# Last parts of experts in quarters of a block, three shared blocks in place of four, in a fused attention and mixture-of-experts kernel

## The chip, the cores and the metric

One core of a Trainium2 chip runs the whole program. The metric is the device time of one execution in microseconds; a profiled execution gives the span from the first to the last instruction and the time of each instruction. Engines are called TensorE (PE; its weight loads are the row PEld), VectorE (DVE), ScalarE (ACT), GpSimd (POOL) and the queue of SyncE (SP).

## What is computed

Two steps are joined. The first is a linear attention with a sketched polynomial kernel, for 4 batches, 4 heads, 1088 positions and a head size of 32: with `phi(x)` the 64 products of two 8-number sketches of `x`, each position gets `phi(q) (sum phi(k) v) / (phi(q) sum phi(k) + 1e-6)`. The heads of a position side by side are a row of 128 numbers, and there are 4352 rows.

The second step sends each row to one of 8 experts:

```python
logits = xn @ en.T / tau                     # xn, en: rows and expert embeddings of length 1
expert_idx = np.argmax(logits, axis=1)
gate_w = probs[np.arange(N), expert_idx]     # probs: softmax of the logits
for e in range(E):
    mask = expert_idx == e
    h = np.maximum(x[mask] @ w1[e], 0.0)     # 128 -> 1024
    out[mask] = gate_w[mask, None] * (h @ w2[e])   # 1024 -> 128
```

So which rows go to which expert is known only while the program runs.

## The kernel before, in words

**Attention.** Batches are handled in two pairs (`m` = 0, 1). Their rows and logits (136 numbers a row) are written to a scratch area in device memory. The steps of the second pair are laid between the first blocks of the experts.

**Blocks.** The rows of an expert are gathered into blocks of 128 (`fetch`, L927: an indirect DMA that GpSimd issues, with row numbers `dst_i` worked out on the chip) and scattered into the output after the two layers (L1032). A block has one expert, whose first-layer weights (512 KB) SP's queue loads with the expert's number read from memory (`weights`, L949); the second layers of all experts lie in `w2_sb`. Ten blocks (`EARLY`) are planned from the first half of the rows, the rest (`LATE`) when all rows are known.

**Shared blocks.** An expert's rows are rarely a multiple of 128. An expert whose last part has at most 64 rows takes only half a block; blocks with the numbers 30 to 33 (`FULL` = 30, `SHARED` = 4) can hold the halves of two experts. They are computed with both experts' weights: `two(i)` (L956) says which they are, `first_b` and `second_b` are the second expert's weights (the second layer is copied by ScalarE, L971).

- `up(i)` (L976) multiplies the turned block (features x rows) by the first layer. A full block takes 8 matmuls of 128 x 128 x 128, a shared one four per `f`: for each of the two experts (`b`) and each half `c` of the 128 hidden numbers, 64 array columns, moving the 64 rows of that expert (L989).
- `turn(i)` (L934) turns a gathered block on TensorE.
- `down(i)` (L1014) adds up 8 matmuls with 128 hidden numbers each. The block's rows are the array columns here. A shared block takes two per `f`, 64 array columns each, one for each expert (L1023).

Float32 matmuls stand in the profile as two instructions each.

**The plan.** `plan_late` (L848) finds for each expert how many whole blocks it has (`full`, a rounded sum from TensorE) and whether a half is left (`odd`), counts the blocks, gives each block a key, and `table` (L775) turns keys into row numbers: TensorE adds up marks, VectorE reduces them (L817). The rows of second halves are moved down 64 partitions by a small matmul (`halves`, L809).

**Order.** The order is written out by hand. `put_at(tick)(after, rank, f)` puts a step `f` at a tick and a rank in it; `emit` (L1125) issues them so on TensorE, VectorE, ScalarE, GpSimd and SP alike. A tick `i` has `up(i)`, `turn(i + 1)` and `down(i - 1)`, in this order on TensorE (`in_ticks`, L1099). 36 blocks (`USUAL`) are always computed. A conditional part at the end (L1141) computes more, up to `NBLK` = 38, if the count read from memory says so. The profile has 36 gathers (L930), so it was not run.

The lines that the change touches lie in the constants at the top, `more_constants`, `iotas`, the handling of the sketch words (L198 to L216), `plan_late`, `table`, `up` and `down`:

Of the kernel before, what the change touches and what calls it, by code (L numbers as in the profile page):

```python
# [33 lines left out]
NBLK = ((N + E * (HALF - 1)) // HALF + 1) // 2  # L34
# [17 lines left out]
LATE = NBLK - EARLY  # L52
SHARED = E // 2
PAIRS = FULL - EARLY
AHEAD = 4
USUAL = N // P + 2
# [9 lines left out]
def kernel(  # L66
# [131 lines left out]
    def word(name):  # L198
        return consts.tile([2 * R, D], U32, name=name)
    top, rem, w, fits = word("s_top"), word("s_rem"), word("s_w"), word("s_fits")  # L200
# [10 lines left out]
    srow = consts.tile([2 * R, D], F32, name="srow")  # L211
# [3 lines left out]
    srows = consts.tile([2 * R, H, D], F32, name="srows")  # L215
# [30 lines left out]
    before, ones = consts.tile([P, P], BF16, name="before"), consts.tile([P, P], BF16, name="ones")  # L246
    less, more = consts.tile([P, E], BF16, name="less"), consts.tile([P, E], BF16, name="more")
    near = consts.tile([P, E], BF16, name="near")
    down_half = consts.tile([HALF, P], BF16, name="down_half")
    base = consts.tile([P, E], BF16, name="base")  # L250
# [10 lines left out]
    nowhere = [consts.tile([P, 2, n], BF16, name=f"nowhere{n}") for n in (EARLY, LATE + SHARED)]  # L261

    def more_constants():
        nc.vector.memset(ones, 1.0 / P)
        nc.vector.memset(ones_e, 1.0)

        nc.vector.memset(less, -(P - 1) / (2.0 * P))
        nc.vector.memset(more, (P - 1) / (2.0 * P))

        nc.vector.memset(near, -1.0 / (2.0 * P))  # L270
        nc.vector.memset(c_early, 0.0)
        nc.vector.memset(w_late, float(KEYS * E))
        for t in (place_k, place_r):
            nc.vector.memset(t, -1.0)
        for t, n in zip(nowhere, (EARLY, LATE)):
            nc.vector.memset(t, 0.0)
            nc.vector.memset(t[:, 0, :n], float(NOWHERE))

    def iotas():
        li = work.tile([P, P], I32, tag="iota", bufs=2, name="lane_i")  # L280
        nc.gpsimd.iota(li[:], pattern=[[1, P]], base=0, channel_multiplier=0)
        nc.vector.tensor_copy(lane, li)
        part = iota([P, 1], [[1, 1]], 0, 1, "part")
        nc.vector.tensor_scalar(before, lane, part[:, 0:1], 1.0 / P, op0=ALU.is_gt, op1=ALU.mult)
        nc.vector.tensor_scalar(down_half, lane[:HALF], part[:HALF, 0:1], float(HALF), op0=ALU.subtract, op1=ALU.is_equal)
        nc.vector.tensor_scalar_mul(lanes, bview(lane, [[1, P], [0, WIDE]]), 1.0 / P)

        nc.vector.tensor_scalar_mul(prefer, lane[:, :E], -1.0 / (2 * E))  # L290
        nc.vector.tensor_scalar_mul(base, lane[:, :E], float(KEYS))
        tok_i = work.tile([P, 3, NM * NCP], I32, tag="iota", bufs=2, name="tok_i")
        toks = tok_i[:, 0].rearrange("p (m c) -> p m c", m=NM)
        for i in range(2):
            nc.gpsimd.iota(toks[:, :, i * NK:(i + 1) * NK], pattern=[[-2 * S, NM], [-1, NK]], base=NOWHERE - S * i,
                           channel_multiplier=-NK)
        nc.gpsimd.iota(toks[:, :, 2 * NK:], pattern=[[-2 * S, NM], [0, 2]], base=NOWHERE - SK, channel_multiplier=-1)

        nc.vector.tensor_scalar(toks[HALF:, :, 2 * NK:], toks[HALF:, :, 2 * NK:], S - HALF, None, op0=ALU.subtract)
        nc.vector.tensor_scalar(tok_i[:, 1], tok_i[:, 0], ~(P - 1) & 0x7FFFFFFF, None, op0=ALU.bitwise_and)  # L300
        nc.vector.tensor_scalar(tok_i[:, 2], tok_i[:, 0], P - 1, None, op0=ALU.bitwise_and)
        nc.vector.tensor_scalar_mul(digits, tok_i[:, 1:], -1.0)
# [439 lines left out]
    SIZES = (EARLY, LATE)  # L742
# [3 lines left out]
    exp_i = [consts.tile([1, n], I32, name=f"exp_i{i}") for i, n in enumerate((EARLY, LATE + SHARED))]  # L746

    def blocks(which, upto, weight, place):

        n = SIZES[which]  # L750
        le = work.tile([P, n, E], F32, tag="le", bufs=2, name=f"le{which}")
        at = consts.tile([P, n + which * SHARED], F32, name=f"at{which}")[:, :n]
# [22 lines left out]
    def table(which, m1, key):  # L775
# [3 lines left out]
        n, w = SIZES[which] + which * SHARED, m1 * NCP  # L779
# [5 lines left out]
        def find():  # L785
            shape = [P, 3 * w * n]
            both = consts.tile(shape, BF16, name="hits0") if which == 0 else work.tile(
                [P, NC * ROW * 2], BF16, tag="xg0", bufs=1, name="hits1")[:, :3 * w * n]
            s["hit"] = both[:, :w * n].rearrange("p (w n) -> p n w", n=n)
            s["col"] = both[:, w * n:].rearrange("p (w d n) -> p d n w", d=2, n=n)  # L790
            nc.vector.tensor_tensor(out=lie(s["hit"]), in0=lie(key().unsqueeze(2).broadcast_to([P, n, w])),
                                    in1=lie(bview(place_k, [[0, n], [1, w]])), op=ALU.is_equal)
# [12 lines left out]
        def first_rows():  # L805
            s["b"] = consts.tile([HALF, 2, SHARED], BF16, name="halves")
            nc.vector.tensor_copy(s["b"], s["ps"].rearrange("p (d n) -> p d n", d=2)[:HALF, :, LATE:])

        def halves():  # L809

            ps = s["ps"].rearrange("p (d n) -> p d n", d=2)
            nc.tensor.matmul(ps[:, :, PAIRS:PAIRS + SHARED], down_half, s["b"], start=False, stop=True, skip_group_check=True)
# [7 lines left out]
    def tokens_by_expert(rounded, out, ps):  # L820

        for j, r in enumerate(rounded):
            for i, t in enumerate([r] + counts):
                nc.tensor.matmul(ps[:, j * E:(j + 1) * E], ones, t, start=i == 0, stop=i == len(counts))
        nc.vector.tensor_scalar(out, ps, WHOLE, -WHOLE, op0=ALU.add, op1=ALU.add)

    def plan_early():
# [3 lines left out]
        def count():  # L831
            tokens_by_expert((less,), full, spare[0][:, NC * E:(NC + 1) * E])
# [15 lines left out]
    def plan_late():  # L848
# [4 lines left out]
        full, all_ = both[:, :E], both[:, E:]  # L853
        odd, odds, rank, key = column("odd"), column("odds"), column("odd_rank"), column("odd_key")
# [3 lines left out]
        def count():  # L858
            tokens_by_expert((near, more), both, table_bank[0][:, 1, :2 * E])
# [15 lines left out]
        def shared():  # L875

            s["high"] = column("high", w=SHARED)
            nc.vector.tensor_sub(odd, all_, full)
            nc.vector.tensor_tensor_scan(out=odds[:], data0=ones_e[:], data1=odd[:], initial=0.0, op0=ALU.mult, op1=ALU.add)
            nc.vector.tensor_scalar(rank, odd, -(NO_KEY + 1), NO_KEY, op0=ALU.mult, op1=ALU.add)  # L880
            nc.vector.tensor_add(rank, rank, odds)

            nc.vector.tensor_scalar(pairs, odds[:, E - 1:], 0.5, 0.25, op0=ALU.mult, op1=ALU.add)
            nc.vector.tensor_scalar(pairs, pairs, WHOLE, -WHOLE, op0=ALU.add, op1=ALU.add)
            nc.vector.scalar_tensor_tensor(out=key, in0=full, scalar=-NO_KEY, in1=base, op0=ALU.add, op1=ALU.add)
            n = 2 * SHARED
            is_it = work.tile([P, n, E], F32, tag="emb", bufs=2, name="is_it")
            it = work.tile([P, n, E], F32, tag="emb", bufs=2, name="it")
            s["keys"] = column("odd_keys", w=n)
            nc.vector.tensor_tensor(out=is_it, in0=bview(rank, [[0, n], [1, E]]),  # L890
                                    in1=bview(lane, [[1, n], [0, E]]), op=ALU.is_equal)
            nc.vector.tensor_mul(it, is_it, bview(key, [[0, n], [1, E]]))
            nc.vector.reduce_sum(out=s["keys"][:], in_=it, axis=AX.X)

        def others():
# [5 lines left out]
            halves = s["keys"][:].rearrange("p (n u) -> p n u", u=2)  # L901
            late["second"] = column("second_keys", w=SHARED)[0:1]
            late["keys"] = whole
            nc.vector.tensor_scalar_add(whole[:, LATE:], halves[:, :, 1], NO_KEY)

            nc.vector.tensor_tensor(out=late["second"], in0=whole[0:1, LATE:], in1=last[0:1], op=ALU.min)
            nc.vector.scalar_tensor_tensor(out=last, in0=halves[:, :, 0], scalar=NO_KEY, in1=last, op0=ALU.add, op1=ALU.min)
            late["key"] = whole

        def experts():  # L910
# [5 lines left out]
            nc.vector.tensor_scalar_min(exp_i[1], f, float(E - 1))  # L916
            late["n"] = consts.tile([1, 1], I32, name="n_late")
            nc.vector.tensor_add(late["n"], pairs[0:1], upto[0:1, E - 1:])
        return count, rest, shared, others, experts
# [4 lines left out]
    def of(i):  # L924
        return (0, i) if i < EARLY else (1, i - EARLY)
# [32 lines left out]


# [16 lines left out]
    def up(i):  # L976
# [3 lines left out]
        for u in range(2):  # L980
            for j in range(4):
# [4 lines left out]
                for b, wh in enumerate((w, first_b(i))):  # L986
                    for c in range(2):
                        r = slice(c * HALF, (c + 1) * HALF)
                        nc.tensor.matmul(ps[r, u, j * P + b * HALF:j * P + (b + 1) * HALF],  # L989
                                         wh[:, f * P + c * HALF:f * P + (c + 1) * HALF], x[:, b * HALF:(b + 1) * HALF],  # L990
                                         start=True, stop=True)
# [22 lines left out]
    def down(i):  # L1014
# [3 lines left out]
        for f in range(NF):  # L1018
# [3 lines left out]
            for b, w in enumerate(ws):  # L1022
                nc.tensor.matmul(ps[b * HALF:(b + 1) * HALF], h[:, f * P + b * HALF:f * P + (b + 1) * HALF], w[:, f],  # L1023
                                 start=f == 0, stop=f == NF - 1, skip_group_check=True)
# [54 lines left out]
    count, rest, shared, others, experts = plan_late()  # L1079
# [7 lines left out]
    put(2, 75.5, experts)  # L1087
    put(3, 73.5, find)
# [50 lines left out]
    n_late = nc.values_load(late["n"][:, :], min_val=0, max_val=LATE,  # L1139
                            skip_runtime_bounds_check_because="a count of blocks, of which there are no more")  # L1140
    with tc.If(n_late > USUAL - EARLY):  # L1141
        put = put_at(-1)
        for i in range(USUAL, NBLK):
            put(0, 0, lambda i=i: fetch(i))
            if i < USUAL + 2:
                put(0, 1, lambda i=i: weights(i))
        put(0, 2, lambda: turn(USUAL))
        in_ticks(USUAL, NBLK, 0)
# [31 lines left out]
```

## Time and profile before

| | |
|---|---|
| median of 3 runs | 202.54 us (202.13 to 202.78) |
| the profiled execution's own time | 204.43 us |
| its span, first to last instruction | 202.6 us |
| TensorE busy | 192.7 us, 95% of the span |
| VectorE, ScalarE, GpSimd busy | 87.6, 102.4 and 107.0 us |
| share of TensorE in the chain that ended last | 90% |
| granted TensorE clock | 1.0 |
| moved by DMA | 39.42 MB, 195 GB/s on average |

The page gives for each engine the time in which it was busy. The chain of work that ended last is followed back from the last instruction, at each step to what released it or to the instruction before it on its engine; its shares tell which engine set the end. Group lines have the line of the source, the engine, the operation, what it writes and reads, the count, and the mean time of one. A matmul's mean is its latency: matmuls overlap, so that the step from one start to the next, which the timeline shows, is the price of one more.

The blocks of the experts run from 55 us to 198 us of the span, a little under 3.7 us each where they are full. The shared ones run from 171.5 us to 193 us.

### The profile page before, as it was taken

Reading aid. Unit: us, or ns where it says so; the run is one execution under the profiler, and the core shown is the slowest. Engines: PE = TensorE matmul, PEld = TensorE weight load, DVE = VectorE, ACT = ScalarE, POOL = GpSimd, SP = SyncE. Lnnn points to the kernel's source line nnn. Section 1 sums busy time; section 2 is a strip of 40 time slices with the busy share of each in tenths; the row PEclk is TensorE's granted clock in tenths of the full one; section 3 lists DMA queues with packets and bytes.
Section 4 is the critical chain, followed back from the end, with each engine's and each line's share of the span. In section 5 each row is a group of like instructions: output and inputs, shape, how many; then the busy total and the mean of one; then the engine's idle time right before and its main releaser. Section 6 shows DMA issues by size and latency. Waiting matters only on the chain.

```text
span 202.6 us, 6949 instructions
## 1 busy us (share of the span) xinstructions
PE 192.7 (95%) x2586; PEld 182.7 (90%) x2586; DVE 87.6 (43%) x378; ACT 102.4 (51%) x293; POOL 107.0 (53%) x137
## 2 busy tenths in 40 slices
PE   7889999999799999999999999999999999999991
PEld 7667888889689999999999999999999999988991
DVE  6677848888658488912222212222122122112200
ACT  2657451436464456434655546545555465766540
POOL 4000335303813767755878777677676776664043
PEclk9999999999999999999999999999999999999999
DMA  4998799987284886544466665657646784485000
GB/s 132 323 217 287 179 320 293 280 282 208 54 321 139 278 310 211 165 132 145 148 205 189 170 205 155 209 166 163 222 147 184 223 306 169 136 263 190 3 26 25
DMA packets 28162, 39.42 MB, mean 195 GB/s; under 512 B 5738, under 2 KB 21366, under 8 KB 28130
## 3 DMA queue, kind: packets, MB, share of 16 engines
q1 hardware_dynamic: 25776, 34.23, 55.9%
q0 software_dynamic: 2304, 4.74, 7.5%
q8 instruction: 22, 0.36, 0.7%
q14 instruction: 10, 0.08, 0.1%
q10 hardware_dynamic: 50, 0.01, 0.0%
HBM read 34.37 MB, written 4.73 MB: 193 GB/s over the span
## 4 chain that ended last, share of the span: by engine, by line
PE 90%; DVE 4%; ACT 2%; issue 1%; DMA 1%; POOL 0%; POOLq 0%; DVEq 0%
PE ps_big L984 28%; PE ps_ab L1020 14%; PE ps_acc L1020 13%; PE ps_big L613 5%; PE ps_acc L479 4%; PE ps_big L989 4%; PE ps_t L382 3%; PE ps_t L936 2%; PE ps_ab L401 2%; PE ps_big L561 2%; PE ps_acc L1023 2%; PE ps_ab L1023 2%; PE ps_t L802 2%; ACT qpT L570 1%; PE ps_ab L591 1%
## 5 line engine op out<-in xcount | busy, mean ns | idle before, releaser
L984 PE MATMUL ps_big<-xTb,wb 128*128 128x128 f32 x512 | 63.0, 276 | 1.6 <-ACT xTb L938 1.4
L984 PEld LDWEIGHTS ps_big<-xTb,wb 128*128 128x128 f32 x512 | 59.7, 192 | 2.4 <-ACT xTb L938 1.6
L1032 POOL DMA_INDIRECT out_dram<-y,dst_i x36 | 37.7, 1048 | 42.9 <-ACT y L1029 24.4
L992 ACT ACTIVATE hT<-ps_big 128x1024 f32<-128x1024 f32 x36 | 36.9, 1024 | 41.3 <-issue 22.7
L930 POOL DMA_INDIRECT xs<-rows,dst_i x36 | 37.3, 1035 | 18.8 <-DVE dst_i L817 11.3
L938 DVE COPY xTb<-ps_t 128x128 f32<-128x128 f32 x29 | 8.4, 290 | 59.4 <-issue 38.2
L1020 PE MATMUL ps_ab<-w_sb,hT 128*128 x256 | 31.3, 275 | 0.0
L1020 PE MATMUL ps_acc<-w_sb,hT 128*128 x256 | 31.2, 275 | 0.0
L1020 PEld LDWEIGHTS ps_ab<-w_sb,hT 128*128 128x128 f32 x256 | 29.9, 192 | 0.0
L1020 PEld LDWEIGHTS ps_acc<-w_sb,hT 128*128 128x128 f32 x256 | 29.9, 192 | 0.0
L998 POOL TENSOR_TENSOR norm<-norm,half_c 128x1 f32<-128x1 f32 x36 | 21.6, 604 | 4.5 <-ACT sq L997 4.1
L1011 DVE TENSOR_SCALAR gate<-gate 128x1 f32<-128x1 f32 x36 | 5.5, 152 | 23.2 <-ACT probs L1008 16.4
L1029 ACT ACTIVATE y<-ps_ab,gate 128x128 f32<-128x128 f32 x17 | 6.2, 367 | 11.0 <-PE ps_ab L1020 6.4
L1029 ACT ACTIVATE y<-ps_acc,gate 128x128 f32<-128x128 f32 x18 | 6.6, 366 | 9.9 <-PE ps_acc L1020 6.8
L1008 ACT ACTIVATE probs<-xs,norm 128x8 f32<-128x8 f32 x36 | 10.6, 295 | 1.2 <-DVE norm L1001 1.2
L997 ACT ACTIVATE sq<-xs 128x128 f32<-128x128 f32 x36 | 10.8, 301 | 0.2
L936 PE MATMUL ps_t<-ident,xs 128*128 128x128 f32 x36 | 10.2, 282 | 0.2 <-issue 0.2
L417 POOL TENSOR_TENSOR kp<-both 128x1024 f32<-128x1024 f32 (+1 forms) x4 | 6.5, 1624 | 7.0 <-ACT both L412 4.8
L479 PE MATMUL ps_acc<-v,kp 128*64 128x64 f32 x256 | 9.2, 225 | 0.5 <-issue 0.5
L319 POOL TENSOR_TENSOR emb_ss<-emb_ss,half_c 8x1 f32<-8x1 f32 x1 | 0.6, 576 | 17.1 <-ACT emb_sq L318 17.1
L479 PEld LDWEIGHTS ps_acc<-v,kp 128*64 128x64 f32 x256 | 8.2, 138 | 1.5 <-issue 1.5
L989 PE MATMUL ps_big<-xTb,wb 128*64 128x64 f32 x128 | 8.3, 224 | 0.3 <-issue 0.2
(254 smaller groups left out, 293.7 us busy)
## 6 DMA issues: line engine op xcount, KB each, us to landing
wb<-in_moe_w_dram SPq DMA_DIRECT2D x36, 512.0 KB
w_sb<-in_moe_w_dram SPq DMA_DIRECT2D x16, 256.0 KB
rows<-xg SPq DMA_DIRECT2D x4, 544.0 KB
v<-in_v_dram SPq DMA_DIRECT2D x4, 512.0 KB
v<-in_moe_w_dram SPq DMA_DIRECT2D x4, 512.0 KB
k<-in_k_dram SPq DMA_DIRECT2D x3, 512.0 KB
q<-in_q_dram SPq DMA_DIRECT2D x3, 512.0 KB
xs<-rows,dst_i POOLq DMA_INDIRECT x36
```

The lines of the kernel that those rows point to most:

```text
L479: nc.tensor.matmul(acc[m][u * HALF:(u + 1) * HALF, i, p], s["kp"][:, c - c0, h], bass.AP(tensor=vo.tensor, offset=vo.offset, ap=[list(vo.a ...
L930: nc.gpsimd.indirect_dma_start(out=xs[i][:], out_offset=None, in_=rows[:2 * S if t == 0 else N + 1], in_offset=bass.IndirectOffsetOnAxis(a ...
L936: nc.tensor.transpose(ps[:, :P], xs[i][:, :DM], ident)
L984: nc.tensor.matmul(ps[:, u, j * P:(j + 1) * P], w[:, f * P:(f + 1) * P], x, start=True, stop=True)
L989: nc.tensor.matmul(ps[r, u, j * P + b * HALF:j * P + (b + 1) * HALF], wh[:, f * P + c * HALF:f * P + (c + 1) * HALF], x[:, b * HALF:(b + 1 ...
L992: nc.scalar.activation(hT[i], ps, ACT.Relu)
L997: nc.scalar.activation(sq, xs[i][:, :DM], ACT.Square, accum_out=norms[i])
L998: nc.gpsimd.tensor_tensor(out=norms[i], in0=norms[i], in1=half_c, op=ALU.pow)
L1008: nc.scalar.activation(p, xs[i][:, DM:], ACT.Exp, scale=norms.pop(i)[:, 0:1], accum_out=gate[i])
L1020: nc.tensor.matmul(ps, h[:, f * P:(f + 1) * P], ws[0][:, f], start=f == 0, stop=f == NF - 1)
L1029: nc.scalar.activation(y, ps, ACT.Copy, scale=gate.pop(i)[:, 0:1])
L1032: d = nc.gpsimd.indirect_dma_start(out=out[:, :], out_offset=bass.IndirectOffsetOnAxis(ap=dst_i[t][:, j:j + 1], axis=0), in_=y[:], in_offs ...
```

## The change

The last part of an expert is counted in quarters of a block (32 rows). A part of over 96 rows is a whole block of its own (the constant `near`), the others have one to three quarters. Experts are ranked by the size of their last part. Six of them go into three shared blocks (`SHARED` = 3), ranks 0, 1, 2 as second expert beside ranks 4, 5, 3. In the first two (`MIXED` = 2) the rows of the first expert are rows 0 to 31 and those of the second 32 to 127; in the third the cut is at 64, as before. A part that doesn't fit is put down as `over` and goes to the conditional part, which is written anew: nine blocks (`EXTRA`), with a table of its own. `USUAL` is 35.

With it come more constants (`fours`, `order`, `down_quart`, `last_first`), and the words of the sketches use buffers of the working pool in place of own ones. In `up`, the four matmuls of an `f` stand in another order, left and right halves of the array in turns of (first expert, left), (second, right), (first, right), (second, left). In `down`, a block cut at 32 takes three matmuls per `f`: array columns 0 to 31, 32 to 63 and 64 to 127.

The core of the diff:

```diff
-NBLK = ((N + E * (HALF - 1)) // HALF + 1) // 2
-LATE = NBLK - EARLY
-SHARED = E // 2
-USUAL = N // P + 2
+USUAL = N // P + 1
+LATE = USUAL - EARLY
+QUART = P // 4
+SHARED = 3
+MIXED = 2
+RANKS = (4, 5, 2, 0, 1, 3)
+SPILL = 3
+EXTRA = SPILL + E - 2
...
     def more_constants():
         nc.vector.memset(ones, 1.0 / P)
+        nc.vector.memset(fours, 4.0 / P)
...
-        nc.vector.memset(more, (P - 1) / (2.0 * P))
-        nc.vector.memset(near, -1.0 / (2.0 * P))
+        nc.vector.memset(more, (QUART - 1) / (2.0 * P))
+        nc.vector.memset(near, -(HALF + 1) / (2.0 * P))
+        for i, rank in enumerate(RANKS):
+            nc.vector.memset(order[:, i:i + 1], float(rank))
...
+        nc.vector.tensor_scalar(down_quart, lane[:P - QUART], part[:P - QUART, 0:1], float(QUART), op0=ALU.subtract, op1=ALU.is_equal)
+        nc.vector.tensor_scalar(last_first, lane[:, :E], -1.0, float(E - 1), op0=ALU.mult, op1=ALU.add)
...
         def halves():
             ps = s["ps"].rearrange("p (d n) -> p d n", d=2)
-            nc.tensor.matmul(ps[:, :, PAIRS:PAIRS + SHARED], down_half, s["b"], start=False, stop=True, skip_group_check=True)
+            for down, a, b in ((down_quart, 0, MIXED), (down_half, MIXED, SHARED)):
+                nc.tensor.matmul(ps[:, :, PAIRS + a:PAIRS + b], down, s["b"][:down.shape[0], :, a:b],
+                                 start=False, stop=True, skip_group_check=True)
...
         def shared():
             s["high"] = column("high", w=SHARED)
-            nc.vector.tensor_sub(odd, all_, full)
-            nc.vector.tensor_tensor_scan(out=odds[:], data0=ones_e[:], data1=odd[:], initial=0.0, op0=ALU.mult, op1=ALU.add)
-            nc.vector.tensor_scalar(rank, odd, -(NO_KEY + 1), NO_KEY, op0=ALU.mult, op1=ALU.add)
-            nc.vector.tensor_add(rank, rank, odds)
-            nc.vector.tensor_scalar(pairs, odds[:, E - 1:], 0.5, 0.25, op0=ALU.mult, op1=ALU.add)
-            nc.vector.tensor_scalar(pairs, pairs, WHOLE, -WHOLE, op0=ALU.add, op1=ALU.add)
+            nc.vector.scalar_tensor_tensor(out=parts, in0=full, scalar=-4.0, in1=quarters, op0=ALU.mult, op1=ALU.add)
+            nc.vector.tensor_scalar_min(odd, parts, 1.0)
+            score = column("score")
+            nc.vector.scalar_tensor_tensor(out=score, in0=parts, scalar=float(E), in1=last_first, op0=ALU.mult, op1=ALU.add)
+            ahead = work.tile([P, E, E], F32, tag="emb", bufs=2, name="ahead")
+            nc.vector.tensor_tensor(out=ahead, in0=bview(score, [[0, E], [1, E]]), in1=bview(score, [[1, E], [0, E]]),
+                                    op=ALU.is_gt)
+            nc.vector.reduce_sum(out=rank, in_=ahead, axis=AX.X)
+            nc.vector.reduce_sum(out=pairs, in_=odd, axis=AX.X)
+            nc.vector.tensor_scalar_min(pairs, pairs, float(SHARED))
+            nc.vector.scalar_tensor_tensor(out=over, in0=parts, scalar=2.0, in1=rank, op0=ALU.mult, op1=ALU.add)
+            nc.vector.tensor_scalar(over, over, float(E - 1), None, op0=ALU.is_gt)
...
+    def cut(i):
+        return QUART if i < FULL + MIXED else HALF
...
     def up(i):
-                for b, wh in enumerate((w, first_b(i))):
-                    for c in range(2):
-                        r = slice(c * HALF, (c + 1) * HALF)
-                        nc.tensor.matmul(ps[r, u, j * P + b * HALF:j * P + (b + 1) * HALF],
-                                         wh[:, f * P + c * HALF:f * P + (c + 1) * HALF], x[:, b * HALF:(b + 1) * HALF],
-                                         start=True, stop=True)
+                for b, c in ((0, 0), (1, 1), (0, 1), (1, 0)):
+                    r = slice(c * HALF, (c + 1) * HALF)
+                    n0, n1 = ((0, cut(i)), (cut(i), P))[b]
+                    nc.tensor.matmul(ps[r, u, j * P + n0:j * P + n1],
+                                     (w, first_b(i))[b][:, f * P + c * HALF:f * P + (c + 1) * HALF], x[:, n0:n1],
+                                     start=True, stop=True)
...
     def down(i):
-            for b, w in enumerate(ws):
-                nc.tensor.matmul(ps[b * HALF:(b + 1) * HALF], h[:, f * P + b * HALF:f * P + (b + 1) * HALF], w[:, f],
-                                 start=f == 0, stop=f == NF - 1, skip_group_check=True)
+            for n0, n1 in ((0, cut(i)), (cut(i), HALF), (HALF, P)):
+                if n0 < n1:
+                    nc.tensor.matmul(ps[n0:n1], h[:, f * P + n0:f * P + n1], ws[int(n0 > 0)][:, f],
+                                     start=f == 0, stop=f == NF - 1, skip_group_check=True)
...
     with tc.If(n_late > USUAL - EARLY):
-        put = put_at(-1)
-        for i in range(USUAL, NBLK):
-            put(0, 0, lambda i=i: fetch(i))
-            if i < USUAL + 2:
-                put(0, 1, lambda i=i: weights(i))
-        put(0, 2, lambda: turn(USUAL))
-        in_ticks(USUAL, NBLK, 0)
+        find, high, low, sums, tokens, *_ = table(2, NM, lambda: late["extra_key"])
+        for f in (extra, find, high, low, sums, lambda: tokens(0, EXTRA)):
+            put_at(-1)(0, -1, f)
+        for i in range(USUAL, USUAL + EXTRA):
+            put_at(max(i - USUAL - AHEAD, -1))(0, 0, lambda i=i: fetch(i))
+            if i < USUAL + 2:
+                put_at(-1)(0, 1, lambda i=i: weights(i))
+        put_at(-1)(0, 2, lambda: turn(USUAL))
+        in_ticks(USUAL, USUAL + EXTRA, 0)
         emit()
```

The new functions `ranked` (the three operations that pick keys by rank, as in `shared` before), `number` (the count of blocks, moved to tick `TABLE1 + 6`) and `extra` (the plan of the conditional part) are left out here.

## The prediction

> **What bounds the kernel now.** I read the page first: busy shares, then the chain of work that ended last.
>
> ```profile
> PE 192.7 (95%) x2586; PEld 182.7 (90%) x2586; DVE 87.6 (43%) x378; ACT 102.4 (51%) x293; POOL 107.0 (53%) x137
> ...
> PE 90%; DVE 4%; ACT 2%; issue 1%; DMA 1%; POOL 0%; POOLq 0%; DVEq 0%
> ```
>
> TensorE holds 90% of the chain; no other engine is near it. So a change counts by what it takes from or adds to TensorE's stream, unless it makes TensorE wait. Next I read the chain in order of time where the shared blocks run (columns: start us, length us, what).
>
> ```profile
> 169.70 1.79 PE ps_acc L1020 x16
> ...
> 180.58 1.86 PE ps_big L989 x64
> 182.45 0.16 issue
> 182.61 0.33 PE ps_t L936
> 182.93 1.90 PE ps_ab L1023 x32
> 184.83 1.86 PE ps_big L989 x64
> 186.69 0.26 PE ps_t L936
> 186.96 1.90 PE ps_acc L1023 x32
> 188.85 1.98 PE ps_big L984 x16
> ```
>
> One turn of the block loop is up (L984, or L989 when shared), the turn of the next block (L936) and down of the block before (L1020, or L1023 when shared). In a shared block two half-width matmuls run side by side, so 64 up instructions take 1.86 us where 16 full ones take 1.79. A whole shared turn is 184.83 - 180.58 = 4.25 us, the next 188.85 - 184.83 = 4.02.
>
> The timeline of TensorE shows single starts, and what a change between full and half-width tiles costs:
>
> ```profile
> 188.35 0.27 PE L1023 MATMUL ps_acc<-w_sb,hT 128*64 x1
> 188.36 0.27 PE L1023 MATMUL ps_acc<-v,hT 128*64 128x128 f32 x1
> 188.46 0.27 PE L1023 MATMUL ps_acc<-w_sb,hT 128*64 x1
> 188.47 0.27 PE L1023 MATMUL ps_acc<-v,hT 128*64 128x128 f32 x1
> 188.57 0.27 PE L1023 MATMUL ps_acc<-w_sb,hT 128*64 x1
> 188.58 0.27 PE L1023 MATMUL ps_acc<-v,hT 128*64 128x128 f32 x1
> 188.78 0.94 PE L984 MATMUL ps_big<-xTb,wb 128*128 128x128 f32 x6
> ```
>
> Each float32 matmul is two instructions (passes). The two halves start 0.01 us apart, pairs follow each other every 0.109 us (188.36, 188.47, 188.58), but the first full-width instruction starts 0.20 us after the last pair: about 0.09 us of nothing. Entering half width costs a further wait: the first pair of the down at 186.88 is followed at 187.04, after 0.16 us, not 0.11, since the first weights could not be loaded ahead.
>
> [...] It has no place where two tiles of different width on *separate* columns follow one another, and that is what this change makes. [...] loads of 128 columns take 192 ns, of 64 columns 137 to 138 ns, so 54 ns for 64 columns. [...] The trace shows order kept between tiles of equal length only.
>
> **Does the fast path still hold?** Routing the reference's inputs gives 524, 552, 568, 587, 623, 527, 504, 467 rows per expert. Modulo 128: 12, 40, 56, 75, 111, 15, 120, 83. Over 96 counts as a whole block, so 32 whole blocks; the other six are 1, 2, 2, 3, 1, 3 quarters. Ranked and paired 3+1, 3+1, 2+2 they fill three shared blocks. 35 in all; the conditional part is skipped. The nearest limit is 8 rows away (56 against 64).
>
> **Part by part.**
>
> *One shared block fewer.* The loop has 35 turns, not 36, and a shared one goes: the mean of 4.25 and 4.02 (chain) is 4.1 us; taken from the same turns by first up instruction, 4.25 and 4.12. I take **-4.2 us**. With it go two loads of weights on SP's queue, a gather and a scatter on POOL and a copy on ACT (L971, 1.04 us), all beside TensorE: nothing more.
>
> *Down of the two mixed blocks (cut at row 32).* Now three matmuls per f: columns 0-31, 32-63 and 64-127 of the array, each moving 128 columns. The built program gives the first two tiles of 128x32 and the third one of 128x64: another mode, sixteen changes per block. If that drains, one f is: two passes of the 32-wide pair, a change, two passes of the 64-wide one, a change. Start to start: 0.16 (pass to pass after a change into 64 columns, 186.88 to 187.04) + 0.21 (last pass to first of the other mode, 188.57 to 188.78) + 0.13 (as 0.16, with half of the 0.054 us of loading saved at 32 columns) + 0.21 = 0.71 us, against 2 x 0.109 = 0.22 now. 8 x (0.71 - 0.22) = 3.9 us per block, **+7.8 us** for two. Lower bound: the three tiles all overlap and an f stays 0.22 us: 0. Between: they take turns without a drain, 8 x 0.22 = 1.75 per block, +3.5. A gain is excluded: each tile alone needs the 0.109 us per pass. I take the drain, [...] since in the trace a change of mode also stops the loading of weights ahead, which the array otherwise does from one instruction to the next.
>
> *Up of the two mixed blocks.* Same 64 instructions, now moving 32 or 96 columns, in the order (left 32, right 96), (right 32, left 96). A half-width pass moving 64 takes 0.058 us (1.86 / 32 pairs). Moving 96 it takes about 0.084, from 0.109 - 0.058 = 0.051 more for 64 columns, so 0.026 for 32[...]. If the halves run on their own: 8 x 2 x (0.058 + 0.084 - 2 x 0.058) = +0.42 us per block. If starts keep program order, the left 96 waits behind the right 32, which waits for the right 96: the two runs of 96 don't overlap, an f takes 4 x 0.084 = 0.336 against 4 x 0.058 = 0.232, +0.83. Not under 0: no column is saved. I take the middle, 0.62: **+1.2 us** for two (0.8 to 1.7, down to 0 if the loads don't bind).
>
> *The third shared block* is cut at 64 as before; only the order of its four up matmuls differs, in equal lengths: 0 (if the left-right order mattered, 0.4 at most, as above).
>
> *Start.* VectorE gets nine more memsets. Before the sketch words arrive it is idle:
>
> ```profile
> 2.00 0.08 DVE L277 MEMSET nowhere<- 128x28 bf16 x1
> 2.45 0.21 DVE L201 TENSOR_SCALAR s_w<-swords 16x32 uint32<-16x32 uint32 x1 [0.37 <-DMA swords<-in_S_dram]
> ```
>
> 0.37 us cover most of the 128x128 one (0.11) and six of one column (0.02 to 0.09 each); three others now stand between the operations on the sketch words (0.07 each, on the chain until 5.04). **+0.2 us** (0 to 0.4). down_quart and last_first come after the sketches, beside TensorE's work.
>
> *Late plan.* Where the shared keys are made, 15 VectorE operations replace 10 (0.15 to 0.25 each, with starts 0.07 to 0.25 apart), two more count the blocks, and the three table operations shrink from 1152 to 1008 elements (1.36 us each, so -0.17 each). About +0.5 us on VectorE, in whose queue the gates and norms stand behind it. The cover:
>
> ```profile
> 84.56 1.34 DVE L795 TENSOR_TENSOR hits<-hits,digits 128x1152 bf16<-128x1152 bf16 x1
> ...
> 87.65 0.15 DVE L1011 TENSOR_SCALAR gate<-gate 128x1 f32<-128x1 f32 x1 [1.49 <-ACT probs L1008]
> ```
>
> TensorE reads the table at 87.84, 1.9 us after 85.90: cost 0 while the growth is under that; were the cover gone, the 0.5 would be paid once. The second row shift (K = 96, then 64) is one more small matmul beside L812: **+0.1 us** on TensorE. The count moved later is read only at the end.
>
> *Buffers:* the sketch words move into working buffers whose next users come over 15 us later: 0.
>
> Sum: -4.2 + 7.8 + 1.2 + 0.2 + 0.1 = +5.1 us. The profiled execution, whose span is 202.6 us and own time 204.43 (1.8 around it), would have a span of 207.7. The median of the runs shown, 202.54, is 1.9 us below that one's own time and equals its span; the same difference on it gives **207.6 us**.
>
> **The rivals.**
>
> *A, the forecast:* mixed widths drain. 205.7 (the drain costs 0.09 us alone, so 32 x 0.09 = 2.9 us on top of taking turns, 3.5; and the up 0.8: -4.2 + 6.4 + 0.8 + 0.2) to 208.5 (all upper ends, the turn at 4.02: -4.0 + 7.8 + 1.7 + 0.4 + 0.1). Chance 0.58.
>
> *B, the other side, faster:* [...] tiles of different width on separate columns overlap, as four row groups by two halves do at L561 (32 instructions moving 256 columns in 1.1 us). Down stays at 1.9 us: -4.2 + 0 + 1.2 + 0.3 = -2.7, so 199.8 us (198.4 with the up at 0 and the start at 0, 200.7 with all upper ends). It decides as soon as a change of width costs less than 0.08 us (2.7 us over 32 changes). For it: all pairs in the trace overlap perfectly. Against: all of them have one width. Chance 0.30.
>
> *C, turns without a drain:* the 64-wide matmul waits for the 32-wide pair but no longer: -4.2 + 3.5 + 1.2 + 0.3 = +0.8, so 203.3 (202.3 to 204.2). For it: order kept; against: the gap at 188.78. Chance 0.10.
>
> *D, the change doesn't do what it says:* a rounded count passes a limit, and the nine blocks of the conditional part run, at 3.69 us each (chain, L984 + L936 + L1020) over 233 us. The 8 rows of margin speak against it: 0.02.
>
> **How the numbers follow.** A measurement of this kernel can tell about 0.3% (0.6 us) from no change. Faster: B, 0.30. Same: C's lower part, 0.04. Slower: A, D and the rest of C, 0.66. The likeliest case gives 207.6, with its own range 205.7 to 208.5. Range for 8 in 10: 199.2 to 208.5, all of A and C and most of B.
>
> **What would show it.** One-to-one by the steps: 35 gathers at the line of L930; up of a mixed block 2.3 to 2.7 us in the chain (B and C the same); down of a mixed block 5.7 us (A), 3.5 (C) or 1.9 (B), with starts of 32-wide and 64-wide matmuls 0.20 us apart in the timeline under A and 0.01 under B; the third shared block still at 1.86 and 1.90. First sketch transpose (L224) at 5.3 to 5.7 us. I am wrong if the down keeps 1.9 us, or if a wait on VectorE or on weights shows up ahead of the shared blocks.

## The result

The changed kernel takes **208.14 us** (median of 6 runs, 206.47 to 208.90) against **202.24 us** (6 runs, 202.01 to 202.78) for the kernel before on the same chip: a ratio of **1.027 [1.023, 1.030]**, slower. The forecast was 207.6. Medians are over all executions listed; ratios leave out those in a slower state, which some executions fall into.

The profiled execution of the changed kernel has an own time of 208.90 us and a span of 207.1 us, at a granted clock of 0.995. Page of after, the lines that answer to the two shown first:

```profile
PE 197.1 (95%) x2522; PEld 182.1 (88%) x2522; DVE 87.8 (42%) x391; ACT 99.6 (48%) x286; POOL 104.6 (51%) x134
PE 92%; DVE 2%; ACT 2%; issue 1%; POOL 0%; POOLq 0%
```

TensorE still carries the chain. It issues 64 instructions fewer and is busy 4.4 us longer (192.7 to 197.1). The page also has 35 gathers and 35 scatters, so the conditional part is skipped and the forecast's case D is out.

The chain of waits of after, in order of time, through the three shared blocks (start us, length us, what; L1042 is the up and L1077 the down of a shared block):

```profile
171.39 2.38 PE ps_big L1042 x40
...
175.84 2.37 PE ps_big L1042 x40
178.22 0.28 PE ps_t L986
178.50 5.49 PE ps_acc L1077 x47
183.98 0.06 PE ps_big L1042
184.04 0.10 PE ps_acc L1077
184.14 1.86 PE ps_big L1042 x62
186.00 0.26 PE ps_t L986
186.26 5.64 PE ps_ab L1077 x48
...
193.99 1.90 PE ps_acc L1077 x32
```

The two long pieces are the downs of the mixed blocks: 184.14 - 178.50 = 5.64 us (the 0.06 between belongs to the next up) and 5.64; a shared down took 1.90 before. The third shared block, cut at 64, has its 1.90 as before. The ups of the mixed blocks take 2.38.

The timeline of TensorE shows one f of a mixed down (a long group merges what overlaps; a second, narrow window shows the 64-wide pair on its own, in the second fence):

```profile
178.43 0.30 PE L1077 MATMUL ps_acc<-w_sb,hT 128*32 x1
178.43 0.30 PE L1077 MATMUL ps_acc<-v,hT 128*32 128x128 f32 x1
178.56 0.27 PE L1077 MATMUL ps_acc<-w_sb,hT 128*32 x1
178.57 0.64 PE L1077 MATMUL ps_acc<-v,hT 128*32 128x128 f32 x3
179.13 0.30 PE L1077 MATMUL ps_acc<-w_sb,hT 128*32 x1
```

```profile
178.77 0.43 PE L1077 MATMUL ps_acc<-v,hT 128*64 128x128 f32 x2
```

The 32-wide pair passes at 178.43 and at 178.56. The first 64-wide pass starts at 178.77, 0.20 to 0.21 us after the last 32-wide one. The two 64-wide passes end together at 179.20 (178.77 + 0.43); with 0.27 for one pass the second started at about 178.93. The next 32-wide pair starts at 179.13, 0.20 later. That is 0.13 + 0.21 + 0.16 + 0.20 = 0.70 us from f to f, where the forecast had 0.71.

**Where the spans part.** They differ by 207.1 - 202.6 = 4.5 us, in three stretches:

| stretch | before | after | difference |
|---|---|---|---|
| start to first up of a shared block | 171.42 | 171.32 | -0.10 |
| from there to VectorE's last y | 27.01 | 30.16 | +3.15 |
| last y to the end | 4.21 | 5.60 | +1.39 |

The middle is the forecast's place. The last row isn't in the forecast at all. The medians lie further apart than the spans, by 5.9 us: before's profiled execution lay 2.2 us above its median, after's 0.8 above its own. The start of the first shared up, which no experiment below touches, came anywhere from 169.65 to 172.69 us in the profiles shown here; so the stretches of one kernel are better compared from there on, and the whole by ratios.

### The profile page after: what moved, and what is told of

Same layout as the page of the kernel before. It is cut to its first block, busy times and chain, and to the rows that moved or that the text cites. A ratio compares the mean times of both kernels' runs of the same rounds, so it can differ in the third digit from the quotient of the medians.

```text
span 207.1 us, 6805 instructions
## 1 busy us (share of the span) xinstructions
PE 197.1 (95%) x2522; PEld 182.1 (88%) x2522; DVE 87.8 (42%) x391; ACT 99.6 (48%) x286; POOL 104.6 (51%) x134
## 4 chain that ended last, share of the span: by engine, by line
PE 92%; DVE 2%; ACT 2%; issue 1%; POOL 0%; POOLq 0%
PE ps_big L1037 27%; PE ps_ab L1073 14%; PE ps_acc L1073 13%; PE ps_big L625 5%; PE ps_acc L491 4%; PE ps_t L394 4%; PE ps_acc L1077 4%; PE ps_big L1042 3%; PE ps_ab L1077 3%; PE ps_ab L413 2%; PE ps_t L986 2%; PE ps_big L573 2%; PE ps_t L815 1%; PE ps_acc L109 1%; ACT qpT L582 1%; PE ps_big L603 1%
## 5 line engine op out<-in xcount | busy, mean ns | idle before, releaser
L1086 POOL DMA_INDIRECT out_dram<-y,dst_i x35 | 36.8, 1052 | 47.9 <-ACT y L1083 24.4
L1045 ACT ACTIVATE hT<-ps_big 128x1024 f32<-128x1024 f32 x35 | 35.8, 1024 | 39.8 <-PE ps_big L1037 38.3
L980 POOL DMA_INDIRECT xs<-rows,dst_i x35 | 36.7, 1048 | 18.7 <-DVE dst_i L832 11.3
L1051 POOL TENSOR_TENSOR norm<-norm,half_c 128x1 f32<-128x1 f32 x35 | 20.8, 597 | 3.5 <-ACT sq L1050 3.1
L396 ACT COPY qT<-ps_t 128x512 f32<-128x512 f32 (+1 forms) x10 | 5.2, 535 | 6.8 <-PE ps_t L394 6.0
```

The costliest lines, as they stand in the source:

```text
L980: nc.gpsimd.indirect_dma_start(out=xs[i][:], out_offset=None, in_=rows[:2 * S if t == 0 else N + 1], in_offset=bass.IndirectOffsetOnAxis(a ...
L1045: nc.scalar.activation(hT[i], ps, ACT.Relu)
L1051: nc.gpsimd.tensor_tensor(out=norms[i], in0=norms[i], in1=half_c, op=ALU.pow)
L1086: d = nc.gpsimd.indirect_dma_start(out=out[:, :], out_offset=bass.IndirectOffsetOnAxis(ap=dst_i[t][:, j:j + 1], axis=0), in_=y[:], in_offs ...
```

## The experiments

The theory (A): tiles of two widths on separate columns take turns, and each change costs a further wait (the forecast's drain). Its rivals: (B) they overlap, (C) they take turns for nothing. Kernels that were measured together share their runs of the kernel before; the medians of those were 202.76, 203.05 and 205.30 us, so kernels of different groups are compared by their ratios.

### Four tiles of one width in the mixed down

```diff
-            for n0, n1 in ((0, cut(i)), (cut(i), HALF), (HALF, P)):
-                if n0 < n1:
+            for n0, n1 in ((0, 32), (32, 64), (64, 96), (96, P)) if cut(i) == QUART else ((0, HALF), (HALF, P)):
...
```

> The down of the two mixed blocks takes four matmuls of 32 array columns each per f, in place of two of 32 and one of 64. All tiles then have one width; there are 16 matmul instructions more per block. If the change of width is what costs (a drain at each of 16 changes), a mixed down falls from 5.6 us to about 1.9 us and the time by 7.5 us, from 208.1 to about 200.6 us. If three or more tiles side by side are slow in themselves (more instructions, each loading its own weights), it stays at 5.6 us or grows to 7 us, and the time stays at 208 us or more.

Measured: 201.02 us (15 runs), ratio 0.992 [0.988, 0.995]. The chain of this kernel:

```profile
176.76 1.88 PE ps_acc L1076 x64
178.64 0.85 PE ps_big L1042 x23
179.49 0.33 issue
179.82 1.39 PE ps_big L1042 x40
...
181.47 1.88 PE ps_ab L1076 x64
```

More instructions (64, not 48), and the down is back at 1.88 us: 3.76 less per block. Its timeline shows all four tiles starting together (x3 is the other three columns), pair after pair; a pass lasts 0.27 to 0.31 us, and the next on its columns starts 0.13 us after it, before it ends:

```profile
176.69 0.30 PE L1076 MATMUL ps_acc<-w_sb,hT 128*32 x1
176.69 0.31 PE L1076 MATMUL ps_acc<-v,hT 128*32 128x128 f32 x3
176.82 0.27 PE L1076 MATMUL ps_acc<-w_sb,hT 128*32 x1
176.83 0.28 PE L1076 MATMUL ps_acc<-v,hT 128*32 128x128 f32 x3
```

So the cost was neither 32 columns as such nor a third tile, but two widths side by side (5.64 us against 1.88). B is out. This one edit makes the changed kernel a little faster than the kernel before (0.8%).

### One change of width inside a block, and seven

The same three tiles per f, but all 32-wide ones first, then all 64-wide ones; and the same with turns every two f.

```diff
-                continue
-            for n0, n1 in ((0, cut(i)), (cut(i), HALF), (HALF, P)):
-                if n0 < n1:
+        for part in (((0, QUART), (QUART, HALF)), ((HALF, P),)) if two(i) and cut(i) == QUART else (((0, HALF), (HALF, P)),) if two(i) else ():
+            for f in range(NF):
+                for n0, n1 in part:
...
```

```diff
-                continue
-            for n0, n1 in ((0, cut(i)), (cut(i), HALF), (HALF, P)):
-                if n0 < n1:
...
+        for f0 in range(0, NF, 2) if two(i) else ():
+            for part in (((0, QUART), (QUART, HALF)), ((HALF, P),)) if cut(i) == QUART else (((0, HALF), (HALF, P)),):
+                for f in (f0, f0 + 1):
+                    for n0, n1 in part:
...
```

> The down of the two mixed blocks keeps its three tiles of 32, 32 and 64 array columns, but all 32-wide matmuls of the eight f come first and all 64-wide ones after them: one change of width inside a block in place of 15. If each change costs about 0.24 us on top of the lost overlap, a mixed down takes 1.8 + 1.8 + 0.3 = about 3.8 us and the time falls by 3.6 us to about 204.5 us. If tiles of two widths were slow however they are ordered, it stays at 5.6 us and 208 us. If tiles of two widths could overlap once the order lets them, it would be near 2 us and 200.6 us.

> As the grouped order of the down of the mixed blocks, but 32-wide and 64-wide matmuls take turns every two f: 7 changes of width inside a block. One change inside gave 3.76 us and 15 gave 5.64, so 0.134 us each; if the price is per change, a mixed down takes 3.76 + 6 x 0.134 = 4.56 us. If the price came from something else in the order (the first pass of each f, say), the down lies off this line by over 0.2 us.

Measured: 204.5 us (8 runs), ratio 1.007 [1.003, 1.011], for the first; for the second one run, 206.98 us beside a median of 205.30 before. The second mixed down in the chain of each:

```profile
183.67 3.76 PE ps_ab L1077 x48
```

```profile
185.16 4.57 PE ps_ab L1078 x48
```

With 15 changes inside the block (as in after) it takes 5.64 us, with one 3.76: (5.64 - 3.76) / 14 = 0.134 us per change. That line gives 3.76 + 6 x 0.134 = 4.56 for 7 changes; 4.57 was measured. The price is also the one that the forecast's 0.71 us for an f implies: (0.71 - 2 x 0.22) / 2 = 0.135. With a single change, 3.76 is still twice the 1.88 of four equal tiles. By itself that doesn't prove that two widths can't overlap, for this order puts all passes of one width ahead of the other, and if passes start about as they are written, there is little left to overlap. That they don't overlap where they stand next to each other is read from the timeline of after: 0.20 us from the start of the last pass of one width to the first of the other, where tiles of one width start 0.01 us apart. So a mixed down's +3.74 is about half loss of overlap (C's part, 1.9) and half changes (A's addition, 14 x 0.134 = 1.9).

### Cut at 64 everywhere

```diff
-        return QUART if i < FULL + MIXED else HALF
+        return HALF
```

This leaves out a part: rows 32 to 63 of the two mixed blocks are multiplied by the other expert's weights. The planning, the 35 blocks and the tail stay.

> The removed turn alone: the two mixed blocks are cut at row 64 in up and in down, so that all three shared blocks run as the third one does. Rows 32 to 63 of these two blocks are multiplied by the other expert's weights, so this part of the result is left out. If the price of the mixed blocks is what makes the kernel slower and one turn less is worth 4.2 us, the time is 202.2 - 4.2 + 1.4 (the longer end, seen in the trace of the changed kernel) = about 199.5 us. If something else in the change costs (start, late plan, waits), it is above 200.5 us.

Measured: 200.1 us (4 runs), ratio 0.987 [0.982, 0.991]. Its chain:

```profile
170.55 2.02 PE ps_big L1042 x64
...
174.61 2.02 PE ps_big L1042 x64
...
176.89 1.90 PE ps_acc L1077 x32
```

This is the change without mixed widths: all that quarters cost beside the matmuls (start, plan, shift, tail) is in it, and it is faster than the kernel before. It also gives what an up of a shared block takes at this place without a wait: 2.02 us. The mixed one takes 2.38 in after, so its unequal lengths cost 0.36.

### What the up of a mixed block waits for

Same matmuls, other order; then the same work in weight tiles of 32 columns, twice as many.

```diff
-                for b, c in ((0, 0), (1, 1), (0, 1), (1, 0)):
+                for b, c in ((0, 0), (0, 1), (1, 0), (1, 1)):
```

> The four up matmuls of a shared block stand in the order of the kernel before (first expert left, first right, second left, second right); all else is the changed kernel. If each half of the array runs its own row of matmuls and a pass of 32 columns is held at 0.058 us by the loading of the next 64 weight columns, order does not matter: a mixed up stays at 2.37 us and the time within 0.5 us of the changed kernel. If the order makes one half wait for the other, a mixed up changes by 0.3 us or more.

```diff
-                for b, c in ((0, 0), (1, 1), (0, 1), (1, 0)):
-                    r = slice(c * HALF, (c + 1) * HALF)
+                for b in range(2):
...
+                    step = cut(i)
+                    for c in range(0, P, step):
+                        nc.tensor.matmul(ps[c:c + step, u, j * P + n0:j * P + n1],
+                                         (w, first_b(i))[b][:, f * P + c:f * P + c + step], x[:, n0:n1],
+                                         start=True, stop=True)
```

> The up of the two mixed blocks takes four tiles of 32 array columns in place of two of 64, so each weight load has 32 columns; twice the instructions, all else is the changed kernel. If the pass of 32 moved columns is held back by its 64-column weight load, a load of half the columns frees it and a mixed up falls from 2.37 to about 1.9 us, the time by 1.0 us. If another floor per instruction holds it, it stays at 2.37 us; if the issue of instructions binds (256 matmul and load records a block), it grows above 2.4 us.

Measured for the order: 208.43 us (4 runs), ratio 1.024 [1.019, 1.029], and an up of 2.40 us; nothing moved. With 32-column weight tiles: 207.7 us (4 runs), 1.023 [1.019, 1.027], and an up of 2.22. In the timeline of after's up, the halves keep their own pace:

```profile
171.33 0.30 PE L1042 MATMUL ps_big<-xTb,v 128*64 128x96 f32 x1
171.40 0.22 PE L1042 MATMUL ps_big<-xTb,wb 128*64 128x32 f32 x1
171.46 0.28 PE L1042 MATMUL ps_big<-xTb,v 128*64 128x96 f32 x2
171.57 0.22 PE L1042 MATMUL ps_big<-xTb,wb 128*64 128x32 f32 x1
171.63 0.28 PE L1042 MATMUL ps_big<-xTb,v 128*64 128x96 f32 x1
```

Passes of 96 columns and of 32 interleave, and an f takes 0.28 us, the forecast's 2 x 0.058 + 2 x 0.084. That is its independent case: the left half doesn't wait for the right one, and the order written is free (2.38 and 2.40 us). But the sum is right rather than its terms, of which the 0.058 for a pass moving 32, the step of one moving 64, was the author's estimate. The starts of one half can be told apart (171.66, 171.69, 171.74, 171.86, 171.94): from a 32-column pass to the next 0.03 us, from there to the first of 96 columns 0.06, then 0.11 and 0.08. With loads of 32 columns these steps are 0.03, 0.03, 0.09 and 0.08, and an f takes 0.23 us; so loads of 64 columns do hold the passes up, by 0.05 us an f. The up gains less than 8 x 0.05 us, for it stops once on the way:

```profile
171.31 0.25 PE L1043 MATMUL ps_big<-xTb,wb 128*32 128x32 f32 x8
171.37 0.38 PE L1043 MATMUL ps_big<-xTb,v 128*32 128x96 f32 x8
171.54 0.46 PE L1043 MATMUL ps_big<-xTb,wb 128*32 128x32 f32 x7
171.81 0.29 PE L1043 MATMUL ps_big<-xTb,v 128*32 128x96 f32 x2
```

The 96-column passes follow the 32-column ones after 0.06 us at 171.31, and after 0.27 at 171.54. All six mixed ups in 32-column tiles (two here, two in each of two kernels below) have such a stop at about 1.2 us after their start, 0.17 to 0.19 us between two starts; its cause stays open. So only 0.16 of the hoped-for half microsecond comes out. In time that isn't resolved (1.023 beside 1.027, with intervals that overlap).

### A shorter conditional part

```diff
-        for i in range(USUAL, USUAL + EXTRA):
+        for i in range(USUAL, USUAL + 2):
...
-        in_ticks(USUAL, USUAL + EXTRA, 0)
+        in_ticks(USUAL, USUAL + 2, 0)
```

The part is skipped in every run here; this one leaves out seven of its nine blocks.

> The conditional part, which is skipped, holds two blocks as before the change, not nine; all else is the changed kernel. If its length makes GpSimd wait for the last scatters where the branches join (and fetch instructions from farther away), the time from the last result of VectorE to the end of the span falls from 5.6 us to about 4.2 us and the time by 1.4 us, to about 206.7 us. If the longer end is chance in one execution (the last scatter landed late), nothing changes: 208.1 us.

Measured: 207.02 us (6 runs), ratio 1.020 [1.016, 1.024], an interval that just touches that of after (from 1.023), so the traces carry this reading. The windows from VectorE's last y to the end, of after and then of this kernel (start:end, length, busy us and instructions of PE, PEld, DVE, ACT and POOL, clock, DMA share, GB/s):

```profile
201.48:207.08 5.60, 0.00 (x0) 0.00 (x0) 0.35 (x1) 0.00 (x0) 0.98 (x1) 0.82 0.10 29
```

```profile
201.26:205.69 4.43, 0.00 (x0) 0.00 (x0) 0.35 (x1) 0.00 (x0) 0.98 (x1) 0.89 0.11 33
```

The same two instructions run in both, the last y and its scatter, yet the end comes 1.17 us earlier with two skipped blocks instead of nine. Before, also with two, had 4.21. The two other kernels with two blocks (below) have 4.4 to 4.5 us, and all eight kernels with nine have 5.6 to 5.9. So the **length of code that isn't run** costs time. The DMA queues in that stretch differ in instruction fetches, first after, then this kernel (packets, MB, share):

```profile
q8 instruction: 2, 0.03, 1.7%
q14 instruction: 3, 0.02, 1.1%
```

```profile
q8 instruction: 1, 0.02, 1.0%
```

In after GpSimd also waits, where the two ways join, until its last scatter has landed, and goes on at 204.97; in the short version it passes the join before that. The semaphores of the two traces split the 1.17 us: the last scatter has landed 3.46 us after the start of the last y in after and 2.87 in the short version, and from there to the end it is 2.13 us and 1.56. So 0.6 us lies before the landing and 0.57 after it. GpSimd's wait fits the second part; why the scatter lands later, by the fetching or otherwise, is not shown.

### Put together

Down and up in 32-column tiles; the same with the short conditional part; and only the down in 32-column tiles with the short conditional part.

> Up and down of the two mixed blocks in tiles of 32 columns; the conditional part stays at nine blocks. If both readings hold, 208.1 - 7.5 - 1.0, and up to 0.5 us back where a block waits for its weights: about 199.9 us, 1.1% faster than before the change. If the two don't add up since waits for weights take their place, about 200.6 us.

> The same as the run with 32-column tiles in up and down, with two blocks in the conditional part in place of nine. If the length of the part that is skipped costs 1.2 us at the end, the time is 1.2 us below that of the other run, about 198.7 us, 1.8% faster than before the change. If the longer end was something else, both runs agree.

> The down of the mixed blocks in tiles of 32 columns, the up as in the changed kernel, and two blocks in the conditional part. If the two gains add up, the ratio to the kernel before is 0.9915 less 0.006 = about 0.985, 199.5 to 200 us. The up in 64-column tiles issues half as many instructions as the 32-column one, so the wait inside the up of the third shared block should be 0.3 us, not 1.2 to 1.7, and the run faster than the one with 32-column tiles in up too. If the ends of the two runs differ only by chance, the ratio is 0.988.

| kernel | median us (runs) | ratio to before |
|---|---|---|
| down and up in 32 | 201.97 (22) | 0.996 [0.994, 0.999] |
| the same, short conditional part | 201.12 (6) | 0.988 [0.983, 0.992] |
| down in 32, short conditional part | 202.44 (6; before beside it 205.30) | 0.985 [0.980, 0.989] |

The last has the lowest ratio, 1.5% under the kernel before, though its interval overlaps with those of the kernel with only the down in 32 tiles and of the one above it. The first two fell short of what was expected, 199.9 and 198.7 us. All three have the down at 1.88 to 1.89 us, and the two short ones tails of 4.44 and 4.45. But something takes part of the gain back. The chain of the last:

```profile
181.86 0.85 PE ps_big L1042 x23
182.71 1.18 issue
183.89 1.39 PE ps_big L1042 x40
```

In the up of the third shared block TensorE stops: for 1.74, 1.22 and 1.18 us in the three kernels in the table's order, and for 0.33 in the first experiment, after 23 recorded instructions each time, with no semaphore named. I had expected about 0.3 in the last one: a miss. Matmuls ahead of the stop already use the weights of both experts, so these had landed. What fits is an instruction fetch: a 16 KB packet on the instruction queue ended 1.2 to 1.5 us before TensorE went on in each (first experiment 178.35 and 179.82, then in the table's order 181.36 and 182.59, 179.50 and 180.74, 182.38 and 183.89). Before has such stops as well, 0.18, 0.14 and 0.16 us; the first ends 1.5 us after such a packet (172.01), but none ended in the 2.5 us before the ends of the other two. After shows no stop; there such packets ended at 179.94 and 186.84, in the mixed downs. That a fetch is the cause is argued, not shown: no run changed it alone, and the cause stays open.

## Why the prediction was right

The direction, what costs (turns, and a wait at each change of width) and its size were right. That the number is only 0.5 us from the median is in part luck: a cost of the tail that was left out made up for costs that were set too high.

- **Down of the mixed blocks**, forecast +7.8 (3.9 each): measured +3.74 each, so +7.5. The sum 0.16 + 0.21 + 0.13 + 0.21 for one f was right to 0.01 us in each of its terms. No pass of one width starts until 0.20 us after the start of the last one of the other, on separate columns too. That the array drains at a change was the author's assumption, and no run shows it, since the profile's ends of matmuls are modelled. What the traces do show is that weights aren't loaded ahead over a change of width: in after the load of the first pass starts with it (both at 178.77, both at 179.13), that of the next pass of the same width 0.11 us ahead of it (178.45 for 178.56); in before likewise (both at 186.88, but 187.05 for 187.15). The runs add that the price goes with the number of changes, 0.134 us each, on top of the lost overlap. Case C described half of the cost. B's condition (a change below 0.08 us) is not met, and it was set wrong: taking turns alone costs 1.9 us per block, as case C's own 3.5 says, so that even a change at no cost would not have made B true.
- **One shared block fewer**, -4.2: the middle stretch agrees. The chains give its +3.15 turn by turn: -4.02 for before's last shared turn, +7.48 for the two downs, -0.08 for the first two ups with the turns after them, and -0.23 in the third shared block, where before had a stop of 0.16 us and a longer turn (0.33 against 0.26).
- **Up of the mixed blocks**, forecast +1.2: mis-sized. The halves are independent (the forecast's lower bound, 0.42; measured 0.36 against the 2.02 us of the same place without a wait). But before's own first two shared ups, from their first piece in the chain to the turn after it, took 2.48 and 2.41 us. They held stops, 0.18 and 0.14 us in the chain; from start to start the stop is longer, 0.41 and 0.36 us where 0.058 is usual, so that it makes up most of the distance from 2.02. After's take 2.38 and 2.38. Net about -0.1. The first of before, in its chain:

```profile
171.49 1.83 PE ps_big L989 x57
173.32 0.18 issue
173.51 0.46 PE ps_big L989 x7
```

  The term compared a new cost with a wait-free row (1.86 us, of a later block) instead of with the rows that it replaces.
- **Start**, +0.2: not resolved. The first block's up starts at 55.24 us, against 55.26 before, but in the kernels of the experiments, which leave the start as it is in after, anywhere from 53.5 to 56.4.
- **Row shift**, +0.1, and **late plan, buffers, third block**, 0: from the first block's up to the first shared one it is 116.16 us before and 116.08 after, so none of them shows a cost; the third down is 1.90 us in both.
- **The tail**, not forecast: +1.39 us. The working read the conditional part as skipped and so as free (case D priced only its being run). Its length went from two blocks to nine, and that is 1.17 us by the short version; the other 0.2 is not accounted for.
- **From span to median**: the sum of +5.1 was set on a median equal to before's span. The spans differ by 4.5, the medians by 5.9; 1.4 us of that is where the two profiled executions lie among their runs, and nothing in the profile says more.

So 5.1 was forecast for the span's 4.5: 0.3 of downs, 1.3 of ups and 0.4 of start and row shift too much, and 1.4 of tail too little. Where the change's gain went is settled: a whole turn of 4.1 us was saved, and more than that (7.5) lost again in the two downs where tiles of two widths alternate; the edit to one width gives the 7.5 back.

## What to carry to other kernels

In these runs tiles on separate columns of TensorE ran together only while they had the same width (a down took 1.88 us with one width, 5.64 with two in turns): where a cut is uneven, split the wider part into more tiles of the narrow width rather than use fewer, wider ones, and if two widths are needed, group them so that they change seldom (3.76 us with one change). Compare a new cost with the row it replaces, at its place, waits included, and not with the cleanest row of the same kind. Code that is skipped still has a length (seven blocks of it took 1.17 us here): look at the tail when a conditional part grows.

## What was not expected of the hardware

- Two tile widths on separate columns don't overlap where they alternate (5.64 us a down, against 1.88 in four tiles of one width), and each further change in a block costs 0.134 us (3.76, 4.57 and 5.64 us with 1, 7 and 15).
- The two halves of the array don't keep a common order where their passes have unequal lengths: an up takes 2.38 us with the halves interleaved and 2.40 in the other order. The timeline shows a 32-column pass of one half beside 96-column ones of the other at their own pace, 0.28 us per f where a common order would give 0.34 by the forecast's sum, an estimate from 0.084 us a pass.
- With narrower weight loads the passes of the mixed up follow each other faster: with moves of 32 and 96 columns an f takes 0.28 us with loads of 64 weight columns and 0.23 with loads of 32. The profile of after has 137 ns and 108 ns for loads of these two widths:

```profile
L1042 PEld LDWEIGHTS ps_big<-xTb,wb 128*64 128x64 f32 x96 | 6.7, 137 | 0.2
L1077 PEld LDWEIGHTS ps_acc<-w_sb,hT 128*32 128x32 f32 x16 | 1.1, 108 | 1.3 <-issue 1.2
```

- Seven skipped blocks of code cost 1.2 us at the end of the kernel.
